# Seven visits of three score units for three groups, with the sums of a pair in one PSUM bank and a word through SyncE between two sets of row tiles

## The chip, the cores and the metric

One core of a Trainium2 chip. The metric is the device time of one execution in microseconds (us), as the median of several; executions of one kernel mostly agree within 1.5%. "Span" is the length of the one execution that was profiled, from its first instruction to its last; it is some 1.8 us shorter than the device time of the same execution.

## The reference

The reference is plain attention with one extra term in the denominator, followed by a feed-forward layer that takes the maximum of three projections.

```python
# q, k, v: 8 batches x 12 heads x 448 positions x 64, float32
scores = scale * np.matmul(q, k.transpose(0, 1, 3, 2))
m = np.max(scores, axis=-1, keepdims=True)
e = np.exp(scores - m)
attn = e / (np.sum(e, axis=-1, keepdims=True) + np.exp(-m) + 1e-09)
attn_out = np.matmul(attn, v)                      # 8 x 12 x 448 x 64
x = attn_out.transpose(0, 2, 1, 3).reshape(3584, 768)
h = np.maximum(np.maximum(x @ w1, x @ w2), x @ w3) # 3584 x 768
return h @ w_out                                   # 3584 x 768
```

## The kernel before

The work is cut into 24 groups of four heads (three groups make a batch). A group has seven score units and two pairs of heads. The kernel walks through *visits*: a visit computes the scores of a few units of one group, then the sums (attention times V) of one pair of the group before, and then fills TensorE with pieces of the projections ("up" pieces, six matmuls each) and of the output matmul ("output" pieces, six matmuls, after every second of which two DMAs to the result are issued on SyncE).

A sequence of 448 is three and a half blocks of 128 and the heads are 64 wide, so part of the matmuls use a 64x64 quadrant of the 128x128 array. Scores are all of that kind ("(row half, column half)" of the array; I call (0,0) and (1,1) diagonal, (0,1) and (1,0) opposite). Of the sums of a pair, 26 are narrow (64x64) and 18 are wide (128x128). PSUM is the memory that matmuls write, and it is divided into banks. Matmuls from the two row halves of the array are kept from adding into one bank at the same time (the prediction names the page that asks for this). The kernel before gives each row half a bank of its own, and joins the two later:

```python
def av_tail(i, ej, pr, ws):                 # narrow sums
    ps = ps_s.tile([128, 2, 512], FP32)     # two banks: index hh, the row half
    for j, w in enumerate(ws):
        for hh in range(2):
            for half in range(2):
                nc.tensor.matmul(out=ps[half*HP : half*HP+HP, hh, j*D1 : (j+1)*D1],
                                 lhsT=eF[hh*HP : hh*HP+HP, o : o+HP],
                                 rhs=vt[hh*HP : hh*HP+HP, pr, 0:D1], ...)

def av_last(i, ej, pr): ...                 # more narrow sums, bank r for row half r
def av_main(i, ej, pr, ws, last):           # wide sums, reciprocal, scale; then
    nc.scalar.activation(out=end, in_=ps[:, 1, 3*D1 : 4*D1], func=AF.Copy)
    def finish():                           # joins the two banks' last column block
        nc.vector.tensor_tensor(out=end, in0=ps[:, 0, 3*D1 : 4*D1], in1=end, op=ALU.add)
        ...
```

```python
visits = ((0, 1), (2, 3), (4, 5, 6))        # units of the three visits of a group
for i in range(3, NI):                      # NI = 24 groups
    transpose_dma(i + 2)                    # q and k transposes, two DMAs on SyncE
    for vi, units in enumerate(visits):
        scores(i, ej, units)
        if vi < 2:
            finish = av(i - 1, pj, vi, ...) # sums of pair vi of the group before
        ...                                 # projection pieces
        if vi == 1:
            x_transpose_dma(i - 1)          # xT<-xn, a DMA on SyncE
        fill(per)                           # more pieces
```

```python
def out_piece(bp, t, c, w, queues):
    ...                                     # six matmuls, evacuation by VectorE
    for half in range(2):
        queues[half].dma_start(out=rows[...], in_=o_sb[...])   # queues = (nc.sync, nc.sync)
```

The softmax here doesn't subtract the row's maximum and nothing guards it: scores larger than these inputs give would overflow.

## Time and profile before

| | kernel before |
|---|---|
| median of 3 executions | 338.45 us (338.43 to 342.95) |
| span of the profiled execution | 336.9 us, TensorE clock 0.999 of full |
| TensorE busy | 97% |
| one visit with two units: first score to first wide sum | 0.727 us |
| changes between 64x64 and 128x128 matmuls in the whole trace | 164, of which 110 after the first 67 us |

The last two rows are read from the start times of single TensorE instructions. In the page, each engine has its busy time and share; in a group line the two numbers after the bar are the group's busy time and the mean length of one instruction in ns, and after the next bar stands the idle time of the engine before such instructions, with what ended most of it. A line of the waits view names an engine and instruction, what it waited for, and then the total in us, how often, and the longest. The prediction below shows and reads the lines that matter; one more is from the view of TensorE's waits. It says that the projection waited once for a transposed xT, 0.3 us:

```profile
PE p_i L490 <- DMA xT<-xn: 0.3, 1, 0.3
```

### The profile page before, as it was taken

Reading aid. Unit: us, or ns where it says so; the run is one execution under the profiler, and the core shown is the slowest. Engines: PE = TensorE matmul, PEld = TensorE weight load, DVE = VectorE, ACT = ScalarE, POOL = GpSimd, SP = SyncE. Lnnn points to the kernel's source line nnn. Section 1 sums busy time; section 2 is a strip of 40 time slices with the busy share of each in tenths; the row PEclk is TensorE's granted clock in tenths of the full one; section 3 lists DMA queues with packets and bytes.
Section 4 is the critical chain, followed back from the end, with each engine's and each line's share of the span. In section 5 each row is a group of like instructions: output and inputs, shape, how many; then the busy total and the mean of one; then the engine's idle time right before and its main releaser. Section 6 shows DMA issues by size and latency. Waiting matters only on the chain.

```text
span 336.9 us, 10248 instructions
## 1 busy us (share of the span) xinstructions
PE 326.1 (97%) x4316; PEld 195.9 (58%) x4316; DVE 199.9 (59%) x521; ACT 183.1 (54%) x289; POOL 146.7 (44%) x260
## 2 busy tenths in 40 slices
PE   7899999999999999999999999999999999999993
PEld 3668788866556655565546646555556555565552
DVE  4556675566566556556656556556556556575552
ACT  4768856655665755676556655666565665420000
POOL 8596578880671539170854328351754000000000
PEclk9999999999999999999999999999999999999999
DMA  8999999799799999969996999989990730124016
GB/s 141 197 200 207 203 205 191 128 161 191 109 108 132 171 234 145 124 96 190 177 156 81 114 259 120 150 99 220 186 149 18 164 89 2 31 47 129 0 33 157
DMA packets 84815, 46.46 MB, mean 138 GB/s; under 512 B 53280, under 2 KB 81312, under 8 KB 84768
## 3 DMA queue, kind: packets, MB, share of 16 engines
q0 software_dynamic: 29120, 21.80, 48.6%
q1 hardware_dynamic: 55264, 23.60, 41.3%
q8 instruction: 34, 0.56, 0.7%
q10 hardware_dynamic: 384, 0.39, 0.4%
q14 instruction: 13, 0.11, 0.1%
HBM read 44.04 MB, written 11.01 MB: 163 GB/s over the span
## 4 chain that ended last, share of the span: by engine, by line
PE 87%; DMA 5%; ACT 2%; DVE 2%; issue 1%; POOL 1%; POOLq 0%; ACTq 0%
PE p_i L490 48%; PE op_ps L514 14%; PE stp L304 11%; PE avp L388 9%; DMA xT<-xn 3%; ACT e L324 2%; DMA ld_q<-in_q_dram 2%; PE avp L344 2%; PE avp L361 1%; DVE xn L404 1%; PE trT L229 1%; DVE QT L190 1%; PE xtp L463 0%; ACT QT L188 0%; DVE rb L401 0%
## 5 line engine op out<-in xcount | busy, mean ns | idle before, releaser
L324 ACT ACTIVATE e<-stp 128x896 f16<-128x896 f32 (+4 forms) x171 | 143.9, 901 | 60.3 <-PE stp L304 60.1
L490 PE MATMUL p_i<-xT,w 128*128 128x448 f16 (+2 forms) x972 | 173.1, 332 | 0.5 <-DMA xT<-xn 0.3
L490 PEld LDWEIGHTS <-w 128*128 128x128 f16 x972 | 90.2, 98 | 69.1 <-issue 6.0
L249 POOL COPY QT<-QT 64x384 f16<-64x384 f16 (+1 forms) x84 | 46.9, 558 | 93.9 <-DMA QT<-ld_q 69.2
L501 DVE TENSOR_TENSOR hT<-hT,p_i 128x448 f16<-128x448 f16 (+2 forms) x96 | 59.7, 622 | 35.7 <-PE p_i L490 35.6
L514 PE MATMUL op_ps<-w,hT 128*128 128x384 f16 (+2 forms) x342 | 58.5, 323 | 0.0
L304 PE MATMUL stp<-QT,KT 64*64 64x448 f16 (+2 forms) x756 | 48.1, 338 | 2.6 <-ACT e L324 0.9
L499 DVE CAST hT<-p_i 128x448 f16<-128x448 f32 (+2 forms) x48 | 30.0, 625 | 25.2 <-PE p_i L490 25.2
L514 PEld LDWEIGHTS <-hT 128*128 128x128 f16 x342 | 32.0, 98 | 22.4 <-issue 2.0
L424 ACT ACTIVATE xn<-end,rl 64x64 f16<-64x64 f32 x72 | 24.9, 346 | 34.5 <-DVE rl L421 34.1
L521 DVE TENSOR_SCALAR o_sb<-op_ps 128x384 f32<-128x384 f32 (+2 forms) x57 | 31.2, 547 | 17.4 <-PE op_ps L514 16.8
L388 PE MATMUL avp<-vx,e 128*128 128x65 f16 x936 | 38.6, 194 | 0.0
L388 PEld LDWEIGHTS <-e 128*128 128x128 f16 x936 | 32.1, 97 | 2.3
L304 PEld LDWEIGHTS <-KT 64*64 64x64 f16 x756 | 15.8, 105 | 26.8 <-issue 23.9
L398 DVE TENSOR_SCALAR rb<-avp 128x6 f32<-128x6 f32 (+2 forms) x54 | 8.8, 164 | 36.8 <-PE avp L388 36.8
L404 DVE TENSOR_TENSOR xn<-avp,rb 128x384 f16<-128x384 f32 (+2 forms) x54 | 29.3, 543 | 1.8
L433 POOL COPY vx<-ld_v 128x768 f16<-128x768 f16 x21 | 17.2, 820 | 6.8 <-issue 4.2
L344 PEld LDWEIGHTS <-e 64*64 64x64 f16 x624 | 13.7, 107 | 8.1 <-issue 1.7
L102 POOL DMA_DIRECT2D ld_q<-in_q_dram x24 | 17.4, 723 | 2.3 <-DMA w<-in_moe_w_dram 1.1
L102 POOL DMA_DIRECT2D ld_k<-in_k_dram x24 | 17.3, 722 | 2.1 <-DMA w<-in_moe_w_out_dram 1.1
L414 ACT ACTIVATE end<-avp 128x65 f32<-128x65 f32 x36 | 8.2, 227 | 17.1 <-PE p_i L490 12.4
L115 POOL DMA_DIRECT2D ld_v<-in_v_dram x24 | 15.2, 634 | 2.6 <-DMA w<-in_moe_w_dram 1.3
(52 smaller groups left out, 162.1 us busy)
## 6 DMA issues: line engine op xcount, KB each, us to landing
out_dram<-o_sb SPq DMA_DIRECT2D x54, 192.0 KB, 4.0
ld_v<-in_v_dram POOLq DMA_DIRECT2D x48, 128.0 KB, 5.1
ld_k<-in_k_dram POOLq DMA_DIRECT2D x23, 224.0 KB, 6.6
ld_q<-in_q_dram POOLq DMA_DIRECT2D x23, 224.0 KB, 7.5
w<-in_moe_w_dram POOLq DMA_DIRECT2D x9, 384.0 KB, 9.2
w<-in_moe_w_out_dram POOLq DMA_DIRECT2D x3, 384.0 KB, 8.5
xT<-xn SPq DMA_TRANSPOSE x18, 4.8
QT<-ld_q SPq DMA_TRANSPOSE x17, 7.3
```

Of the source, the lines that this page charges most:

```text
L102: nc.gpsimd.dma_start(out=tiles[nm][:, 1 : NP * T + 1].rearrange("x (r t) d -> x r (t d)", r=NP)[:, p0:p1], in_=src[:, p0:p1],)
L249: eng.tensor_copy(out=t[d0 : d0 + HP, o * 128 : (o + n) * 128], in_=t[s0 : s0 + HP, a * 128 : (a + n) * 128],)
L304: nc.tensor.matmul(out=stp[half * HP : half * HP + HP, par, j * qn : (j + 1) * qn], lhsT=k_block(i, pr, h2, x[half]), rhs=q_cols(i, pr, h2 ...
L324: nc.scalar.activation(out=dst, in_=src, func=AF.Exp, scale=scale)
L388: nc.tensor.matmul(out=ps[:, hh, j * D1 : (j + 1) * D1], lhsT=eF[:, o : o + 128], rhs=vx[:, 2 * pr + hh, (x[0]), 0:D1], start=False, stop= ...
L404: nc.vector.tensor_tensor(out=xn[i][:, pr, ws[0] : ws[0] + nw].rearrange("p j h d -> p h j d"), in0=acc[:, :, :, 0:D], in1=rb.unsqueeze(3) ...
L424: nc.scalar.activation(out=xn[i][0:HP, pr, 3, hh], in_=end[h, 0:D], func=AF.Copy, scale=rl[h])
L490: nc.tensor.matmul(out=p_i[:, j * qn : (j + 1) * qn], lhsT=w_sb[i][:, dc, ts(fc, 128)], rhs=xT[b][:, dc, q0 : q0 + qn], start=(dc == 0), s ...
L499: nc.vector.tensor_copy(out=dst, in_=src)
L501: nc.vector.tensor_tensor(out=dst, in0=dst, in1=src, op=ALU.max)
L514: nc.tensor.matmul(out=op_ps[:, 0:w], lhsT=hT[bp][:, fc, ts(t, 128)], rhs=wout_sb[:, fc, c : c + w], start=(fc == 0), stop=(fc == NFC - 1),)
L521: nc.vector.tensor_scalar(out=o_sb[:, c : c + w], in0=op_ps[:, 0:w], scalar1=1.0 / LAMBDA, scalar2=None, op0=ALU.mult,)
```

## The change

Intent: save mode changes of the array and work of VectorE and ScalarE. Three groups (21 units) are walked in seven visits of three units, in place of nine of two, two and three. A pair's sums go into *one* PSUM bank, so the join on ScalarE and VectorE falls away. Since both row halves now write one bank, the narrow sums are split: first the diagonal ones, which write different partitions of the bank (they come from both row halves, start in pairs, mostly within 6 ns, and the results of all runs are correct, so the rule that the prediction quotes is wider than these runs needed), then the opposite ones, which must not start before the last diagonal one is done. A matmul can start ahead of an earlier one whose quadrant is taken (the vt, vx, vx, vt rows in the prediction, and run 3), so program order isn't enough; the diff sends a word through another engine: a no-op on SyncE that waits for the last diagonal sum, and for which the first opposite sum waits. The scores of the visit are laid around these two sets to fill the other quadrants meanwhile. The core of the diff (cuts marked):

```diff
+    def visit(units, pair):
+        ...
+        ps = banks[0]
+        def turn_over(mm):
+            turned = nc.sync.nop()
+            tc.add_manual_dep(turned.ins, mm.ins.name, AFTER, reason="PSUM bank")
+            return turned
+        ...
+            (s0, _), (s1, _), (s2, _) = qk
+            for at in diag + anti:
+                s0(*at)
+            for at in anti:
+                s1(*at)
+            turned = turn_over(smalls(diag, True))
+            for at in diag:
+                s1(*at)
+            for at in anti + diag:
+                s2(*at)
+            smalls(anti, False, turned)     # the first of them waits for `turned`
+            for _, power in qk:
+                power()
+            wides()
...
-    for i in range(3, NI):
-        ...
-        for vi, units in enumerate(visits):
-            scores(i, ej, units)
-            ...
+    adds = {NV0 + 3: 1, **{NV0 + 7 * (b - 1) + 1: b for b in range(2, B - 1)}}
+    for n, (units, pair) in enumerate(plan):
+        ...
+            visit([(i, u) for i, us in units for u in us], pair)
+        for i, us in units:
+            if n >= NV0 and us[0] == 0 and i + 2 < NI:
+                transpose_dma(i + 2)
+        ...
+        if n in adds:
+            add_batch(adds[n])
+        if pair and pair[1] == 1 and pair[0] >= 3 * PE_X:
+            x_transpose_dma(pair[0])
+        ...
+        fill(per)
```

Pieces of projection are also placed in the score buffers (`places`), so that more PSUM is open to them.

## The prediction

> **What bounds the kernel now.** I read the page first, then the start times of single TensorE instructions, then SyncE's queue, because the change puts SyncE between two TensorE instructions. From the page:
>
> ```profile
> PE 326.1 (97%) x4316; PEld 195.9 (58%) x4316; DVE 199.9 (59%) x521; ACT 183.1 (54%) x289; POOL 146.7 (44%) x260
> ...
> DMA  8999999799799999969996999989990730124016
> ...
> L304 PE MATMUL stp<-QT,KT 64*64 64x448 f16 (+2 forms) x756 | 48.1, 338 | 2.6 <-ACT e L324 0.9
> ...
> out_dram<-o_sb SPq DMA_DIRECT2D x54, 192.0 KB, 4.0
> ...
> xT<-xn SPq DMA_TRANSPOSE x18, 4.8
> ```
>
> TensorE is never free: 97% busy, and the score matmuls wait 0.9 us in all for an exponential to release a buffer. VectorE and ScalarE have 40% spare, so what the change takes from them is worth nothing by itself. The DMA engines are near full until three quarters of the span; a transposed xT lands a median 4.8 us after its issue. What counts is TensorE time, and every new TensorE wait. One visit in the timeline of TensorE (start, length, group), with the next two starts:
>
> ```profile
> 142.82 0.57 PE L304 MATMUL stp<-QT,KT 64*64 64x448 f16 x8
> 143.22 0.26 PE L344 MATMUL avp<-vt,e 64*64 64x65 f16 x12
> 143.32 0.19 PE L361 MATMUL avp<-vt,e 64*64 64x65 f16 x1
> 143.32 0.20 PE L361 MATMUL avp<-vx,e 64*64 64x65 f16 x2
> 143.33 0.19 PE L361 MATMUL avp<-vt,e 64*64 64x65 f16 x1
> 143.35 0.26 PE L361 MATMUL avp<-vx,e 64*64 64x65 f16 x10
> 143.55 0.74 PE L388 MATMUL avp<-vx,e 128*128 128x65 f16 x18
> 144.13 1.30 PE L490 MATMUL p_i<-xT,w 128*128 128x448 f16 x6
> ...
> 147.10 3.10 PE L514 MATMUL op_ps<-w,hT 128*128 128x384 f16 x18
> 150.13 0.57 PE L304 MATMUL stp<-QT,KT 64*64 64x448 f16 x8
> ```
>
> Two score units (8 matmuls of 64x64) take 0.40 us, the 26 narrow sums 0.33 us, the 18 wide ones 0.58 us. Start to start, instruction by instruction: 189 ns from one 448-column matmul to the next, but 282 ns where the second is a 64x64 score; 162 and 257 ns after 384 columns; 124 ns from the last narrow sum to the first wide, where narrow rounds are 29 ns apart. So a change between 64x64 and 128x128 costs 94 ns, twice a visit, always. The four small L361 rows show a second thing: the program issues vt, vt, then vx; the array starts vt, vx, vx, vt, in all 36 sums. A matmul whose quadrant is taken doesn't hold back one for a free quadrant, which the new order needs.
>
> SyncE's queue and ScalarE over the same stretch:
>
> ```profile
> 147.37 1.23 SPq L473 DMA_TRANSPOSE xT<-xn  x1
> 148.87 3.19 SPq L531 DMA_DIRECT2D out_dram<-o_sb  x4
> 152.24 1.29 SPq L241 DMA_TRANSPOSE QT<-ld_q  x1
> 153.63 3.62 SPq L241 DMA_TRANSPOSE KT<-ld_k  x1
> ```
> ```profile
> 146.64 0.70 ACT L424 ACTIVATE xn<-end,rl 64x64 f16<-64x64 f32 x2 [0.99 <-DVE rl L421]
> ```
>
> SyncE is not an idle messenger. The visit at 150.13 follows an output piece; SyncE issues that piece's two transfers until 148.87 + 3.19 = 152.06, that is 1.93 us into the visit. A transpose holds it 1.2 to 4 us.
>
> **What the Trainium skill says.** "TensorEngine Tiling (Array Packing)", Key Properties: a change of tiling mode drains TensorE. The trace agrees: the 94 ns. The same page, Gotcha 1: row tiles must not access one PSUM bank simultaneously and software must synchronize them. That is why the change needs the word; no run so far shows a violation. "TensorE: Matmul & The Clock Gate", Part 3: matmuls start and end in strict order. The vt, vx, vx, vt rows disagree, and I follow the rows. "Perfetto Trace Analysis", per-instruction lifecycle, hardware-generated DMA: the sequencer waits for the semaphore, then for descriptor generation, and only then is free for its next instruction. The SyncE rows agree (back-to-back issues about 0.6 us apart).
>
> **The change part by part.** From group 6 on there are 54 visits of 2, 2 and 3 units, plus two closing sums: 56 blocks, 112 mode changes. After it, 42 visits of 3 units (37 carry a pair's sums, 5 don't), plus one closing pair that changes four times: 88.
>
> 1. Mode changes: 24 fewer x 94 ns = -2.3 us.
> 2. Packing. Matmul counts don't change: 26 narrow, 18 wide a pair. Before, the narrow ones ran on four quadrants, 8 rounds x 29 = 230 ns; with three units at 190, 800 ns. Now 7 diagonal rounds (203 ns) run beside one half unit and 6 opposite rounds (174 ns) beside another: 190 + 203 + 190 + 190 = 773. Saving 27 ns x 37 = -1.0 us.
> 3. The word, if SyncE is free. The last diagonal sum starts 204 + 6 x 29 = 378 ns into the visit and takes 190 (its row): 568. The opposite quadrants are free at about 580. The way out cost 50 ns elsewhere in this trace (score end to exponential start); SyncE steps are 17 ns with some 50 between; the way back I estimate at 50 more. So the word arrives near 700, 0.12 us late. In the 28 visits not counted in step 4: +3.4 us. The saving is spent here.
> 4. The word, if SyncE is busy. The no-op stands in SyncE's queue behind the previous visit's outputs. Counting pieces with the plan of the diff, nine pair visits (the three early ones with short fills, one a batch after, the closing pair) directly follow an output piece that issues DMAs. There SyncE is free at 1.93 us, against 0.58 when the sums could go: 1.3 us x 9 = +11.7 us, all on TensorE, since the wide sums stand behind.
> 5. The word behind transposes. The diff moves the q and k transposes after the visit's word, so they endanger only the next one. Their two issues take 2.5 to 7 us, a visit about 5.5. Perhaps three overlap by 0.7 us: +2 us.
> 6. xT. A batch's up-projection now starts one visit after its last pair's sums; before, it started three visits after. In this trace the time from the last wide sum to xT landed was 9.7, 10.4, 12.6, 8.0, 7.3 and 6.2 us for the six groups that complete a batch, and the next batch's first matmul came as close as 0.3 us behind it. Now the final scale on ScalarE no longer waits for a piece of projection, -1.1 us. But xT queues on SyncE behind a pair of q/k transposes in the same visit, about +1.5. What lies between on TensorE: four output pieces of 0.97 (six in the first case), scores 0.68, and 0.76 for the four matmuls that don't need the last group: 5.4 us (7.3). The needed wait exceeds that by 2 to 6 us in the first batches and nothing in the late ones, where DMA is quiet. I put down 2 + 3 + 2 + 1 + 0 = +8 us, well below a straight transfer of the old latencies, because a stalled TensorE also thins the traffic.
> 7. VectorE and ScalarE lose a 0.23 us copy, a 0.22 us addition and two 0.16 us steps a pair. Off the path: 0. Projection pieces in score buffers: their exponential ends 1.4 us into the visit, before the wide sums end; 0.
>
> Sum: -2.3 - 1.0 + 3.4 + 11.7 + 2 + 8 = +21.8, about 360 us. Steps 4 and 6 are the large ones and both rest on queues that may shift, so I predict 354.
>
> **The rivals.** (a) The change works as meant: the word is hidden, SyncE is free when needed, xT arrives. Then only steps 1 to 3 stand: 335 to 339 us, the same within 2%. For it: the quadrants start independently, and transposes were moved with care. Against it: SyncE's 152.06. (b) Only SyncE's order hurts, xT doesn't: 350 us. For it: xT leaves earlier after the sums. Against it: landings of 7 us and more while DMA is full. (c) The array does not run a long score and short sums side by side. Then both sets of rounds stand in series, about +0.35 us x 37 = 13 us on top: over 365 us. Against it: the reordered rounds. (d) Fewer stalls for buffers make it faster by over 2%: nothing in the page can be removed to that amount; TensorE's waits are 1 us.
>
> **Range and chances.** Rival (a) gives the lower edge, the full sum with some of (c) the upper: 340 to 367. Slower by over 2% means above 345.2; half of step 4 alone with step 3 nearly gets there. I give 0.75 to slower, 0.19 to within 2%, 0.06 to faster.
>
> **What would show it.** Steps 1 and 2: 282 and 124 ns changes in 42 visits; diagonal sums starting within the first half microsecond beside scores. Step 3: the first opposite sum about 0.7 us into a free visit. Step 4: in nine visits it starts near 2 us, ended by SyncE, with output DMAs just before the no-op. Step 6: the first up-projection of a batch idle before its fifth matmul, waiting for DMA xT. I am wrong if the opposite sums start at 0.6 us also after output pieces, or if TensorE's idle time stays under 13 us.

## The result, and the profile after

The changed kernel took 360.08 us (median of 4, 359.12 to 360.99); the kernel before, in the same rounds, 338.44 us (median of 4, 338.18 to 342.95). The ratio is 1.061, with a 95% interval of 1.051 to 1.070: slower. A ratio here and below is the mean time of one kernel's fast runs over that of the other's in the same rounds, so it is not quite the ratio of the quoted medians. Executions over 1.5% slower than the fastest of the same kernel are left out of the means. The profiled spans are 359.1 and 336.9 us: 22.2 us to explain. (The profiled execution of the changed kernel was the slowest of its four.)

From the page of the changed kernel (engines; the chain that ended last; the group of narrow sums; two DMA issues with KB and median us from issue to landing):

```profile
PE 335.4 (93%) x4324; PEld 201.5 (56%) x4324; DVE 184.3 (51%) x413; ACT 173.4 (48%) x257; POOL 146.4 (41%) x260
...
PE 75%; SPq 10%; DMA 6%; DVE 4%; ACT 2%; issue 2%; POOL 0%; DVEq 0%; ACTq 0%; POOLq 0%
...
L452 PE MATMUL pb<-vt,e 64*64 64x65 f16 x532 | 21.7, 195 | 11.6 <-SPq L472 11.1
...
out_dram<-o_sb SPq DMA_DIRECT2D x54, 192.0 KB, 3.0
...
xT<-xn SPq DMA_TRANSPOSE x18, 3.1
```

Against the kernel before, VectorE and ScalarE lost 108 and 32 instructions, as intended. TensorE fell from 97% to 93% busy, and L472, the no-op on SyncE, is what it waits for: 11.1 us in which the array stood still. SyncE's queue, SPq, makes up 10% of the chain that ended last. And xT now lands 3.1 us after its issue instead of 4.8. TensorE's waits by cause:

```profile
PE pb L452 <- SPq L472: 11.1, 10, 2.8
...
PE pb L588 <- DMA xT<-xn: 1.1, 3, 0.5
```

Now two visits in the timeline of TensorE (start, length, group; in brackets idle time and what ended it). First one in which SyncE was free:

```profile
131.08 0.38 PE L414 MATMUL ps<-QT,KT 64*64 64x448 f16 x4
131.29 0.19 PE L452 MATMUL pb<-vt,e 64*64 64x65 f16 x2
...
131.49 0.57 PE L414 MATMUL ps<-QT,KT 64*64 64x448 f16 x6
131.86 0.28 PE L452 MATMUL pb<-vt,e 64*64 64x65 f16 x6
...
132.17 0.39 PE L481 MATMUL pb<-vx,e 128*128 128x65 f16 x7
```

The scores begin at 131.08; the diagonal sums run from 131.29 beside other scores; the opposite sums begin at 131.86, which is 0.78 us into the visit, and the wide ones at 132.17, 1.09 us in. Averaged over the 27 visits of this kind, on the same scale: last diagonal sum starts 0.406, no-op on SyncE 0.725, first opposite sum 0.786, first wide 1.096. (A 28th, the first visit, has a free word too but a late bank.) Three units of scores and the same sums would have taken 0.727 + 0.190 = 0.917 us in the old form, by my estimate; no run has that form. Between the start of the last score (0.628) and 0.786 TensorE starts nothing: it waits for the word. The semaphore events in the trace (no view prints them) split this wait: the semaphore of the last diagonal sum is raised a median 113 ns after the modelled end of that sum, the no-op runs 17 ns later, and the first opposite sum 61 ns after that. So the messenger itself takes 78 ns, and the larger part is that the sum is reported done late.

Then a visit that follows an output piece, with SyncE's queue over the same stretch:

```profile
238.38 0.38 PE L414 MATMUL ps<-QT,KT 64*64 64x448 f16 x4
...
240.29 0.28 PE L452 MATMUL pb<-vt,e 64*64 64x65 f16 x6 [0.94 <-SPq L472]
```
```profile
239.07 1.11 SPq L629 DMA_DIRECT2D out_dram<-o_sb  x2
240.42 1.26 SPq L259 DMA_TRANSPOSE QT<-ld_q  x1
```

SyncE issues the two DMAs of the output piece until 239.07 + 1.11 = 240.18. Only then does the no-op run (240.23) and only after it the first opposite sum: 1.91 us into the visit instead of 0.79. This happens in eight visits and in the closing pair, nine in all; the first opposite sum starts 2.66, 1.91, 3.75, 2.56, 1.93, 1.91, 1.91 and 1.91 us in, and 1.92 in the closing pair. Against 0.787 the eight lose 12.25 us, the closing pair 0.9.

The longest of them has an aftermath. In two stretches of the windows view (length and busy time of each engine in us with instruction counts, then the granted TensorE clock, DMA share, GB/s), the first is that visit, in which TensorE stands idle 2.78 us at one go, the second what follows:

```profile
82.20:86.30 4.10, 1.32 (x39) 0.77 (x38) 0.56 (x1) 2.54 (x3) 0.00 (x0) 0.98 1.28 123
86.30:89.70 3.40, 3.40 (x31) 1.99 (x27) 0.92 (x3) 0.62 (x2) 0.65 (x2) 0.52 1.29 188
```

TensorE is full in the second stretch, but at a granted clock of 0.52: for 3.41 us its 448-column matmuls start 373 ns apart instead of 189. That costs 1.3 to 1.7 us. It need not be in every execution: the mean granted clock of the four was 0.995 (the profiled one), 0.993, 0.999 and 1.0, and the last two were 1.2 to 1.9 us faster.

The account, from the start times of single instructions. "Predicted" has the steps as the prediction numbers them:

| part | where seen | measured, us | predicted, us |
|---|---|---|---|
| 24 fewer mode changes (164 to 140) x 94 ns | starts | -2.3 | -2.3 (step 1) |
| block of scores and sums, 1.096 against 0.917, x 37 | starts | +6.6 | +2.4 (steps 2 and 3) |
| word late behind output DMAs, nine times | waits, SyncE's queue | +13.2 | +11.7 (step 4) |
| word late behind a q/k transpose, once | waits | +0.4 | +2 (step 5) |
| xT not there: 2.15 us in five places, 0.46 before | waits, starts | +1.7 | +8 (step 6) |
| first visit: the one bank not yet read out | starts | +0.4 | - |
| 3.41 us at half clock | windows | +1.3 or more | - |
| other waits of the projections and outputs | starts | +0.9 | - |
| sum | | +22.2 or more | +21.8 |

The measured difference of the spans is 22.2 us, and up to the end of the last matmul, which is what the table is about, 22.8 (331.6 to 354.4). In the second visit the bank comes 0.7 us late as well, but that lies inside its late word and isn't counted twice. The account is argued from one trace; the experiments have to show that these are causes.

### The profile page after: what moved, and what is told of

Its sections match the earlier page's. It is cut to its first block, busy times and chain, and to the rows that moved or that the text cites. A ratio compares the mean times of both kernels' runs of the same rounds, so it can differ in the third digit from the quotient of the medians.

```text
span 359.1 us, 10352 instructions
## 1 busy us (share of the span) xinstructions
PE 335.4 (93%) x4324; PEld 201.5 (56%) x4324; DVE 184.3 (51%) x413; ACT 173.4 (48%) x257; POOL 146.4 (41%) x260
## 4 chain that ended last, share of the span: by engine, by line
PE 75%; SPq 10%; DMA 6%; DVE 4%; ACT 2%; issue 2%; POOL 0%; DVEq 0%; ACTq 0%; POOLq 0%
PE pb L588 29%; PE ps L588 15%; SPq L259 6%; PE pb L481 6%; PE ps L414 6%; PE pb L612 5%; DMA xT<-xn 4%; PE ps L612 4%; SPq L629 3%; PE pb L452 3%; PE ps L379 2%; PE ps L322 2%; DVE o_sb L619 2%; DMA ld_q<-in_q_dram 1%; ACT e L342 1%
## 5 line engine op out<-in xcount | busy, mean ns | idle before, releaser
L425 ACT ACTIVATE e<-ps 128x896 f16<-128x896 f32 x126 | 106.6, 918 | 106.3 <-PE ps L414 106.2
L588 PE MATMUL pb<-xT,w 128*128 128x448 f16 (+2 forms) x684 | 123.8, 325 | 1.7 <-DMA xT<-xn 1.1
L588 PE MATMUL ps<-xT,w 128*128 128x448 f16 x288 | 59.2, 352 | 0.0
L599 DVE TENSOR_TENSOR hT<-hT,pb 128x448 f16<-128x448 f16 (+2 forms) x65 | 40.4, 621 | 20.4 <-PE pb L588 18.1
L342 ACT ACTIVATE e<-ps 128x896 f16<-128x896 f32 (+4 forms) x45 | 36.4, 869 | 18.8 <-PE ps L322 18.4
L612 PEld LDWEIGHTS <-hT 128*128 128x128 f16 x342 | 32.0, 98 | 22.2 <-DVE hT L599 2.0
L414 PE MATMUL ps<-QT,KT 64*64 64x448 f16 x504 | 40.4, 357 | 0.0
L612 PE MATMUL pb<-w,hT 128*128 128x384 f16 (+2 forms) x198 | 35.7, 321 | 0.4 <-DVE xT L567 0.3
L524 ACT ACTIVATE xn<-pb,rb 64x64 f16<-64x64 f32 x76 | 23.5, 309 | 20.1 <-DVE xn L516 17.8
L452 PE MATMUL pb<-vt,e 64*64 64x65 f16 x532 | 21.7, 195 | 11.6 <-SPq L472 11.1
L481 PE MATMUL pb<-vx,e 128*128 128x65 f16 x684 | 28.4, 195 | 0.0
L612 PE MATMUL ps<-w,hT 128*128 128x384 f16 x144 | 26.1, 326 | 0.0
```

The lines of the kernel that those rows point to most:

```text
L342: nc.scalar.activation(out=dst, in_=src, func=AF.Exp, scale=scale)
L414: return nc.tensor.matmul(out=stp[half * HP : half * HP + HP, par, 0:S], lhsT=k_block(i, pr, h2, x[half]), rhs=q_cols(i, pr, h2, par, "EO" ...
L425: nc.scalar.activation(out=dst, in_=stp[:, :, 0:S], func=AF.Exp, scale=scale)
L452: yield lambda m=m, w=w, o=o, rhs=rhs: nc.tensor.matmul(out=ps[cc, w * D1 : (w + 1) * D1], lhsT=eF[rr, o : o + HP], rhs=rhs, start=start a ...
L481: nc.tensor.matmul(out=ps[:, (3 * hh + j) * D1 : (3 * hh + j + 1) * D1], lhsT=eF[:, o : o + 128], rhs=vx[:, 2 * pr + hh, (x[0]), 0:D1], st ...
L524: nc.scalar.activation(out=dst[0:HP, pr, 3, hh], in_=acc[h, 6, 0:D], func=AF.Copy, scale=rb[h, 6:7])
```

## The experiments

Two theories were to be told apart. Mine: the word is the loss, in two ways: where SyncE is busy it is late, where SyncE is free it still takes longer than the work that was laid beside it. Rival one: the array doesn't run scores and short sums side by side as the change needs. Rival two: late xT is the loss, and the waits for SyncE merely hide it. All outputs are right.

**1. Output DMAs behind the word** (out_behind). The two issues of an output piece are held and sent after the next visit's no-op and xT:

```diff
+            def send(q=queues[half], ...):
+                q.dma_start(out=rows[:, c0:c1], in_=o_sb[...])
+            held.append(send) if hold[0] else send()
-            queues[half].dma_start(out=rows[...], in_=o_sb[...])
...                                          # in the loop over the plan, behind x_transpose_dma
+        let_go()
```

> The output transfers of a visit's pieces are issued on SyncE after the next visit's word and xT transpose, nothing else changes. If the word stuck behind output issues is the large loss (12.5 us of late words in nine visits, plus about 1.2 us of half clock after the longest of them), the nine late words arrive at 0.79 us like the others and the time is 346 us (344 to 349). If the loss lies in the form of the visit itself (packing, buffers, xT), it stays at 357 to 361 us.

Measured 349.66 us (347.65 to 350.68, n 4), ratio to before 1.030 (1.023 to 1.037). No word stands behind output DMAs any more: seven of the nine late ones are on time, one is slightly late (1.15 us), and the second visit still has its opposite sum at 2.47 us, behind a q/k transpose. One more visit is at 1.38. The times from first score to first wide sum, added over the 38 blocks with sums, fall from 54.06 to 43.92 us, 10.1 us; the opposite sums of the closing pair, which this doesn't count, come 0.9 us sooner; and the profile has no half clock (1.3 to 1.7): together 12.3 to 12.7. The last matmul ends 12.3 us sooner (354.4 to 342.1), although the first of these visits begins 0.5 us later; what follows it is 0.8 us longer, so the span fell by 11.5 (359.1 to 347.6). So step 4 of the prediction is shown as a cause. That the half clock hung on the long idle time fits, but isn't shown: two executions of the changed kernel seem to be without it. The run is just outside the expected range, mostly because one late word is left.

**2. Diagonal sums first** (diag_first). Only the order on TensorE, so that the word is sent earlier and more scores lie behind it:

```diff
-            for at in diag + anti:
-                s0(*at)
-            for at in anti:
-                s1(*at)
+            for at in anti:
+                s0(*at)
             turned = turn_over(smalls(diag, True))
             for at in diag:
-                s1(*at)
+                s0(*at)
+            for at in anti + diag:
+                s1(*at)
             for at in anti + diag:
                 s2(*at)
```

> The diagonal sums are issued beside the first half unit of scores instead of the second, so that the word has one more slot of 0.2 us to travel. The order on SyncE is that of the change. If in free visits TensorE waits 0.16 us for the word, the wide sums start at 0.94 us instead of 1.10 us in 28 visits, and the time falls by 4.4 us to 355.5 us (354 to 357); late words stay late. If the 1.10 us come from how the array shares its quadrants, nothing changes: 360 us.

Measured 354.28 us (353.32 to 355.10, n 4), ratio 1.044 (1.038 to 1.051): 5.8 us less than the changed kernel, as expected. In free visits the no-op now runs at 0.529, the opposite sums start at 0.592 and the wide at 0.917 us, the time estimated for the old form; 27 x 0.18 = 4.8 us of the gain are that. The late words stay late (1.91 to 2.86 us), though the one of 3.75 us is now at 1.91. So the wait for the word is the cause of the 0.18 us, and order alone hides it. That the total fits is partly luck: the blocks lose 6.3 us in all and this profile has no half clock, but its waits for xT are 4.6 us instead of 2.15, one of them 2.35. They begin to show here.

**3. Both together** (both).

> Both edits together. The two waits are of different visits or follow each other, so the gains should add: nine late words gone and 37 words hidden, about 18.5 us: 341.5 us (339 to 344). If the gains overlap, 345 us or more.

Measured 344.11 us (343.42 to 346.11, n 4), ratio 1.016 (1.008 to 1.024); whether this is within 2% of before the interval leaves unclear, and it is just outside the expected range (344). The sum of the two single gains is 10.4 + 5.8 = 16.2; together they gave 16.0. The blocks say the same (10.1 and 6.3; together 16.0), so the two losses add. A free visit in the timeline:

```profile
122.04 0.38 PE L414 MATMUL ps<-QT,KT 64*64 64x448 f16 x2
122.05 0.32 PE L452 MATMUL pb<-vt,e 64*64 64x65 f16 x8
...
122.25 0.35 PE L414 MATMUL ps<-QT,KT 64*64 64x448 f16 x2
122.26 0.19 PE L452 MATMUL pb<-vx,e 64*64 64x65 f16 x2
```

The scores at 122.25 start in front of the two sums at 122.26, which the program issues earlier: the quadrants do run on their own. The remaining waits that the kernel before doesn't have: the first two visits' bank (0.52, 1.04 and 0.22 us), VectorE 0.43, one word behind a transpose 1.18, and xT 0.33 + 0.83 + 0.93 + 0.64 + 0.34 = 3.07 us, where it was 2.15 in the changed kernel. The last is what the next runs went for.

**4. Up-projection one visit later** (both_late), so that xT has a visit more to land:

```diff
-    adds = {NV0 + 3: 1, **{NV0 + 7 * (b - 1) + 1: b for b in range(2, B - 1)}}
+    adds = {NV0 + 3: 1, **{NV0 + 7 * (b - 1) + 2: b for b in range(2, B - 1)}}
```

> As the former, and a batch's up-projection is queued one visit later, so that xT has landed. TensorE's waits for xT in the changed kernel sum to 2.1 us; without them 339.5 us (337 to 342). If moving the pieces makes fills uneven and brings other waits, no gain over the former.

Measured 350.70 us (349.18 to 353.12, n 4), ratio 1.035 (1.027 to 1.042): a miss by over 10 us, in the wrong direction. From its waits:

```profile
PE pb L452 <- SPq L472: 6.9, 5, 2.6
...
PE pb L588 <- DMA xT<-xn: 0.2, 1, 0.2
```

The waits for xT are gone, as intended. But where the outputs stand in the plan has moved with the projection, and the word is late again: five times, up to 2.6 us. After that longest idle time come 3.41 us at half clock. The stall was not removed, it was moved from one wait to the other.

**5. xT ahead of the q and k transposes on SyncE** (xt_first), on top of both: the loop with `transpose_dma(i + 2)` stands behind `x_transpose_dma` in the plan loop instead of before it.

> As 'both', with the q and k transposes of a visit issued on SyncE after its xT transpose instead of before. In 'both' they delay the xT issue by 0 to 0.65 us past the finished xn, and TensorE waits 3.1 us in all for xT. If SyncE's order makes that wait, it falls to about 1.5 us and the time to 342.5 us (341.5 to 343.5). If the transfer itself makes it, the time stays at 344 us.

Measured 348.20 us (347.89 to 352.42, n 5), ratio 1.027 (1.019 to 1.035). A miss. xT is issued sooner and its waits fall from 3.07 to 1.3 us, but the q and k transposes now stand with the outputs in front of later words: eight words are late, by 6.9 us on TensorE. The profiled execution was the slowest of the five and has 3.41 us at half clock, after an idle time of 1.985 us.

**6. Three more words** (four_words): on top of both, the no-op is followed by three more, each waiting for the one before.

```diff
             turned = nc.sync.nop()
             tc.add_manual_dep(turned.ins, mm.ins.name, AFTER, reason="PSUM bank")
+            for _ in range(3):
+                again = nc.sync.nop()
+                tc.add_manual_dep(again.ins, turned.ins.name, AFTER, reason="PSUM bank")
+                turned = again
```

> As 'both', with three more no-ops on SyncE between the diagonal sums and the opposite ones. This doubles and more the suspected cost of a free word: each step is some 60 ns by the distance from no-op to sum. In 'both' the word arrives just as the quadrants come free and the opposite sums have about 50 ns to spare, so 36 x (3 x 60 - 50) ns = 4.7 us: 349 us (347 to 351). If a word on SyncE costs nothing while other scores run, no change.

Measured 350.68 us (349.83 to 353.08, n 4), ratio 1.035 (1.027 to 1.043), 6.6 us above both, as expected. The first no-op still runs at 0.529 us; the opposite sums start at 0.79 to 0.84 instead of 0.592, so a step on SyncE costs 66 to 80 ns, and the wide sums at 1.10 to 1.14. That is 0.19 us a block, times 36 is 6.7 us. (The profiled execution was the slowest, 9.0 us above both: words late behind SyncE's queue and 3.41 us at half clock are in it too.) It confirms the size of the word by adding to it, and it says what the order in both is worth: a word that is 0.2 us slower would bring back the whole loss of a free visit.

**7. Output pieces away from the visits with sums** (spread), on top of xt_first: `share` divides by 0.6 visits more, so that more pieces are left for the visit without sums.

```diff
-        return max(0, (left() + sum(sums)) / len(rest) - sums[0])
+        more = 0.6 if n >= NV0 + 3 and nxt < len(plan) else 0
+        return max(0, (left() + sum(sums)) / (len(rest) + more) - sums[0])
```

> As 'xt_first', and two or three output pieces of a batch are left for the visit that has no sums, ahead of the next batch's up-projection, so that xT has landed. Unlike in 'both_late' the visits keep their fills. Waits for xT fall below 0.5 us (but for the last group's 0.35): 341 us (340 to 342.5). If fills become uneven and transfers again stand before a word, 343 us or more.

Measured 348.74 us (347.20 to 349.21, n 4), ratio 1.027 (1.020 to 1.034). A miss: xT no longer waits (0.35 us, at the very end), but six words are late, by 0.5 to 1.6 us. As long as the word shares SyncE with outputs and transposes, the three orders tried only choose who waits.

**8. Nothing side by side** (serial): on top of out_behind, all scores first, then diagonal sums, word, opposite sums.

```diff
             for at in diag + anti:
                 s0(*at)
-            for at in anti:
+            for at in diag + anti:
                 s1(*at)
+            for at in diag + anti:
+                s2(*at)
             turned = turn_over(smalls(diag, True))
-            for at in diag:
-                s1(*at)
-            for at in anti + diag:
-                s2(*at)
             smalls(anti, False, turned)
```

> As 'both', but all three score units first, then the diagonal sums, the word and the opposite sums, so that nothing runs beside them. If the array really runs narrow sums beside scores, this loses the hidden rounds and the whole word: wide sums start near 1.4 us instead of 0.92, 36 x 0.48 = 17 us more: 361 us (355 to 366). If the array ran them one after the other anyway (rival c of the prediction), the wide sums start at most 0.2 us later: under 352 us.

Measured 357.12 us (356.00 to 358.72, n 4), ratio 1.053 (1.045 to 1.061). One visit:

```profile
124.71 0.76 PE L414 MATMUL ps<-QT,KT 64*64 64x448 f16 x12
...
125.42 0.26 PE L452 MATMUL pb<-vx,e 64*64 64x65 f16 x6
125.78 0.28 PE L452 MATMUL pb<-vt,e 64*64 64x65 f16 x6
...
126.09 0.58 PE L481 MATMUL pb<-vx,e 128*128 128x65 f16 x13
```

Here the word's bare gap can be read: the last diagonal sum starts about 125.49 and the first opposite one 0.29 us later at 125.78. In the changed kernel it is 0.38. The messenger takes the same 78 ns in both; what differs is when the sum is reported done, 19 ns after its modelled end here and 113 ns in the changed kernel, where scores run beside it. Why is not shown. The wide sums come 1.38 us into the visit instead of 1.096, and the whole is 7.5 us above out_behind, from which it differs in this order alone, and 13.0 above both. So the change's interleaving does work and is worth 7.5 us over this order, and 13 with the diagonal sums first; rival one falls.

**9. The word through ScalarE** (act_word): the changed kernel with one line changed.

```diff
-            turned = nc.sync.nop()
+            turned = nc.scalar.nop()
```

> The changed kernel with one word replaced: the no-op that hands the word on runs on ScalarE instead of SyncE. Order, transfers, packing and plan stay as in the change. In ScalarE's queue nothing stands before it but a long finished xn. If it is SyncE's queue that costs, the nine late words come at 0.79 us (12.9 us), the half clock goes (1.2 us), free visits stay at 1.10 us: 346 us (344 to 349). If what is waited for is a semaphore between engines as such, nothing changes: 360 us; if holding up the exponentials by 0.3 us a visit matters, above 349 us.

Measured 352.71 us (350.88 to 355.98, n 4), ratio 1.043 (1.036 to 1.049). Better than the changed kernel, but a miss. In the trace every word is on time (opposite sums at 0.797, wide at 1.106 us), there is no half clock, and the 38 blocks sum to 42.6 us. The expectation had a rival for a time above 349 us, that the exponentials are held up; after 73 us no matmul waits over 0.1 us for one. The expected gain was there and was partly given back:

```profile
PE pb L588 <- DMA xT<-xn: 4.8, 5, 1.4
```

Counted from start times the waits for xT rose from 2.15 to 5.57 us. SyncE's queue at the same batch boundary, first in the changed kernel, then here:

```profile
158.93 1.12 SPq L629 DMA_DIRECT2D out_dram<-o_sb  x2
160.30 1.38 SPq L259 DMA_TRANSPOSE QT<-ld_q  x1
...
163.61 1.25 SPq L571 DMA_TRANSPOSE xT<-xn  x1
```
```profile
150.44 1.10 SPq L629 DMA_DIRECT2D out_dram<-o_sb  x2
151.71 1.48 SPq L259 DMA_TRANSPOSE QT<-ld_q  x1
...
154.99 1.25 SPq L571 DMA_TRANSPOSE xT<-xn  x1
```

The queue is the same to 0.2 us. What has moved is TensorE: the last wide sum of the pair starts at 161.01 in the changed kernel and at 151.39 here. Measured from there, xT is issued 2.6 us later in the one and 3.6 us later in the other. In the changed kernel the late word held back the sums too, so that SyncE had a lead when they ended. That is why the wait for xT looked small. ScalarE isn't what holds xT here: xn is ready at 153.81, and the KT transpose leaves SyncE at 154.88. The last matmul ends 10.3 us sooner than in the changed kernel; 11.5 in the blocks, 0.9 in the closing pair and 1.3 to 1.7 for the half clock, less 3.4 for xT, is 10.3 to 10.7, so the account closes. The spread of 5 us among the four executions was not seen in a trace, as only the fastest was profiled.

**10. The word through ScalarE and diagonal sums first** (act_first), so with the edits of 9 and 2.

> As 'act_word', with the diagonal sums beside the first half unit as in 'diag_first'. The wide sums start at 0.92 us in all visits with scores. 36 x 0.18 = 6.4 us less than 'act_word': 340.5 us (338.5 to 343). If delayed exponentials bite, 343 or more.

Measured 348.86 us (347.44 to 353.39, n 4, one of them, 353.39, slow), ratio of fast runs 1.029 (1.026 to 1.032). A miss by 8 us. The wide sums start at 0.917 us in all visits but the first three, so both losses by the word are gone. But:

```profile
PE pb L588 <- DMA xT<-xn: 7.1, 5, 2.3
```

From start times: 1.59 + 2.44 + 1.88 + 1.66 + 0.34 = 7.9 us. This is the size that step 6 of the prediction had put on xT (+8 us): a wait like it is there, it was only not to be seen while the word was late. The sum is nearer than its grounds, though. Step 6 counted on slow transfers; here these transposes land 3.1 to 3.3 us after issue, and the four large waits come from the issue, 3.8 to 4.6 us after the last wide sum, because xT stands on SyncE behind the q and k transposes. There it is issued 1.4, 2.2, 1.8 and 1.6 us after xn is ready, which is nearly each wait. Rival two has its part in this: xT is a loss of its own, behind the first.

**11. All of it** (act_all): act_first, xT ahead of the q and k transposes, output pieces left for the visit without sums, and the change's own order in the first two visits, where the bank is free late:

```diff
+            if late: ...                     # the change's order of scores and diagonal sums
+            else: ...                        # diagonal sums first
-            visit([(i, u) for i, us in units for u in us], pair)
+            visit([(i, u) for i, us in units for u in us], pair, n < NV0 + 2)
```

> An attempt at a version that beats both: as 'act_first', xT's transpose ahead of the q and k transposes, two or three output pieces left over for the visit without sums so that xT lands in time, and the order of the change in the first two visits, whose sums must wait for their bank. Without a word on SyncE these moves should no longer hit a word: waits for xT below 0.5 us, 338.5 us (337 to 340.5), that is the kernel before within 1%. If the accounts of the former runs miss a cause, it stays above 341 us.

Measured 340.91 us (340.35 to 341.48, n 4), ratio 1.007 (1.005 to 1.009): within 2% of before, slower by 0.7%, just above the expected range. No word is late, and no single wait is over 0.8 us. From start times, the blocks of the first three visits are 1.95 us over 0.917 us each (the bank and VectorE), and the waits in projections and outputs come to 2.2 us against 0.9 before; with the mode changes (-2.3) that is about +1.0 us, and up to the end of the last matmul the difference is 0.96 (331.6 to 332.6). The other 0.9 of the 1.9 us between the spans (336.9 to 338.7) lie behind it: from there to the end of the program pass 5.3 us in the kernel before and 6.2 here, for the last evacuation and its DMAs. The run makes three edits to act_first at once, so what each of them is worth stays open. No version that was run beats the kernel before.

## Why the prediction was right

The direction, the time (354 against 360.08) and the range (340 to 367) held, and the sum of its steps before it was shaded, 360, is the measured time. That closeness is partly luck: two parts were wrong by 4 (steps 2 and 3) and 6 us (step 6) in opposite directions, and effects of some 2.6 us together were not in it.

- **Step 1, mode changes, -2.3 us: right.** 24 fewer, counted.
- **Step 2, packing, -1.0 us: wrong, there is no gain.** In the best arrangement (runs 2, 10, 11) the first wide sum comes at 0.917 us, which is what the old form's 0.727 + 0.190 comes to: the interleaving gains nothing over the old packing. The bound there is the diagonal chain of scores: the last starts at 0.636, takes 0.189, and the mode change 0.094.
- **Step 3, the free word, +3.4 us for 28 visits: the right mechanism, the size too small.** I put its arrival near 0.70 us; it was 0.786. The last diagonal sum starts 28 ns later than I had it (0.406 against 0.378). The term that was mis-sized is the way out: 130 ns from the modelled end of that sum to the no-op where I had taken 50 from another pair of engines. It isn't the messenger that is slow: 113 of the 130 ns pass before the sum's semaphore is raised. In run 8, with no scores beside it, the whole way out is 36 ns. The way back was 61 against an estimated 50, so it stands. Steps 2 and 3 together came to 0.18 us x 37 = 6.6 instead of 2.4. Runs 2 and 6 show it as a cause, by removing it and by adding to it.
- **Step 4, the word behind output DMAs, 1.3 us x 9 = +11.7: right.** Nine visits, the predicted ones, 13.2 us. Six of them are at 1.91 to 1.93, where the view of the kernel before had put SyncE's end at 1.93; three are later: in two of them the outputs stand behind q/k transposes (the longest: until 82.97 us, 3.75 us in), in one the two issues take 1.75 us instead of 1.1. Runs 1 and 9 show it as a cause.
- **Step 5, transposes, +2: too large** by 1.6 us in the changed kernel; in runs 3 to 5 the same queue shows it in other visits.
- **Step 6, xT, +8: wrong for this kernel, by 6.3 us.** Two reasons. For the last group of a batch, which is what counts, the landing was faster: 3.0 to 3.3 us after issue, where the kernel before had 4.3 to 9.5 in the first five batches of that kind (other groups' transposes still took up to 8.6). And it was counted beside step 4 though both are the same delay of SyncE: a late word holds back the sums that produce xn, so that xT's place in the queue costs nothing then. With step 4 and the free word gone, 7.9 us of waits for xT are there (run 10), but through SyncE's queue and not through slow landings. The steps of a sum must be worked out one after the other, each on the timeline that the earlier ones leave.
- **Step 7, nothing for VectorE and ScalarE: right;** TensorE's time doesn't fall with their 108 and 32 instructions.
- **Not in the prediction:** the single bank in the first visit (0.4 us; 0.7 more in the second lies inside its late word), the half clock after a long idle time (1.3 us or more), and other waits (0.9 us).
- **The rivals.** (a), all hidden, needs what run 11 does, and even that is 340.9 rather than 335 to 339. (c), nothing side by side, is refuted by the reordered starts in run 3 and by run 8. (b), only SyncE's order hurts, is closest to the trace of the changed kernel, but run 10 shows that xT is only hidden.

## What to carry to other kernels

An engine used as a messenger is a queue: before putting a word through it, list what stands in front of the word in each place, and choose an engine whose queue is empty at that moment, or lay more independent work behind the last producer than the word takes (here about 0.2 us from the producer's modelled end, of which only 0.08 is the messenger, and 1.1 us more where two output DMAs stood in front). When a stall is taken away, look at what it was hiding: here the first fixes gained 10 and 6 us, and three later ones (runs 4, 5 and 7) only handed the wait from one user of SyncE to another. And when a change adds several waits on one engine, don't add them up: a delay that comes first shortens those after it.

## What the Trainium skill lacked or had wrong

- "TensorEngine Tiling (Array Packing)", Key Properties: that a change of tiling mode drains the array is there, but no size. The runs show 94 ns a change (282 instead of 189 ns from one matmul to the next), twice a block.
- "TensorE: Matmul & The Clock Gate": Part 3 has matmuls start and end in strict program order. The traces show 64x64 matmuls for a free quadrant starting ahead of earlier ones for a taken one (run 3: scores at 122.25 in front of earlier sums at 122.26). Part 1 puts the clock's fall after an idle window of about 3.4 us, and the table under "Why this matters for your kernels" asks for gaps under some 3 us; here 3.41 us at half clock followed idle times of 2.78, 2.62, 1.985 and 1.79 us in four runs, while 2.28 us in run 10 and 2.19 in run 2 had no such effect. What decides it was not found.
- No page gives the cost of a word between two matmuls of a kernel through another engine. From the raising of the matmul's semaphore to the no-op it is 17 ns on SyncE (22 on ScalarE), 61 to 67 ns from there to the next matmul, and 66 to 80 ns for each further no-op in a row. Nor does any page give how much later than its modelled end a 64x64 matmul is reported done while others run beside it: the semaphore is raised 97 to 113 ns later beside scores (runs 1 to 3), 19 ns in run 8.
